# Attention and two MoE layers on one core: the activations of five tiles turned in 32x32 blocks by VectorE instead of by TensorE

## Chip, cores and metric

The kernel runs on one core of one Trainium2 chip. The metric is the device time of one execution in microseconds (us). PE is TensorE, PEld its weight loads, DVE VectorE, ACT ScalarE, POOL GpSimd, SP the engine whose queue issues most transfers.

## What is computed

Three layers follow each other (batch 4, 8 heads, 512 local and 32 global positions, head size 64, so 2176 rows of 512):

```
out_g = softmax(scale * q_g @ [k_g, k_l].T) @ [v_g, v_l]              # global rows
s_l   = scale * [q_l @ k_g.T, where(|i - j| <= 32, q_l @ k_l.T, -1e9)] # local rows
out_l = softmax(s_l) @ [v_g, v_l]
x = rows of [out_g, out_l]                       # 2176 x 512

h = x @ w_in                                     # 2176 x 2048
g = maximum(0.01 * h, h)
x = g @ w_out                                    # 2176 x 512

logits = x @ phi                                 # 2176 x 32, 8 experts x 4 slots
d = softmax(logits, axis=0)                      # over all rows
slot_out[e] = maximum((d.T @ x)[e] @ w1[e], 0) @ w2[e]
out = softmax(logits, axis=1) @ slot_out
```

## The kernel before

The rows are worked in 17 tiles of 128 (`NTT`): four per batch, 0 to 15, and tile 16 with the global rows. The attention of a batch (`a_T`, `a_S`, `a_E`, `a_V`, `g_S`, `g_E`, `g_V`) fills `xn`; the MLP of its tiles runs beside the attention of the next batch.

For one tile t the MLP does the following.
- `b_X` (L635) turns x on TensorE and splits it into two parts, `xh` and `xl`.
- `b_H` (L657) makes one slice f of h, 512 of the 2048 columns, by 12 matmuls into a bank `hp` (two banks), and ScalarE's activation writes g (L679).
- `b_L` (L683) turns that slice of g: four transposes on TensorE (L688) into a bank, and one copy (L690) to a tile `gT`. From tile 6 on that copy is ScalarE's.
- `b_M` (L695) multiplies all four `gT` of a tile with `pmat`, which is w_out @ phi made ahead, so that logits come without x @ w_out: 16 matmuls (L700) into one bank `lg`, columns by four row groups.
- `b_D1` copies `lg` to `lp` on VectorE (L709), `b_D2` adds the four groups on TensorE (L715, `lg<-lp`) and takes the running column maximum and exponentials, `b_D3` turns them back (L759, `lg<-identr,st`) and makes the row softmax.
- `b_U` adds d.T @ g to a sum over tiles (`up`, L769; `uacc`, L774).

`l_items(t)` lists the steps after H of one tile, `b_items` weaves those of tile t-1 between the H slices of tile t. Tiles 15 and 16 (`ts`) are done together at the end (`j_M`, `j_D`). The order on each engine is set by the framework's scheduler from the order of the code, from dependences and from a simulated timeline; `tc.issue_after(ins)` adds the edge that what follows is issued after `ins`. The semaphores and the buffers of the pools make the waits. A pool tile with a tag has `bufs` buffers that are used in turn; `reuse_waits="tile"` lets a new tile wait for all users of the one it replaces.

The experts' weights, 33.5 MB, are loaded by `load_next`, in the order of a list `loads`, as buffers come free: eight of pool `xp`, the eight of `wp` (the parts of w_in, each pair free after H of its slice for tile 16), those of `g`, `xn`, `xh` and `xl`. They are used by `layer1` (`ehp`, L1113) and the second layer (`sop`).

Of the kernel before, what the change touches and what calls it, by code (L numbers as in the profile page):

```python
# [20 lines left out]
def kernel(  # L21
# [20 lines left out]
    P = 128  # L42
# [68 lines left out]
    st = actx.enter_context(tc.tile_pool(name="st", bufs=2))  # L111
# [3 lines left out]
    m32 = sb.tile([32, 3, P], F32, tag="gT", name="m32", bufs=4)  # L115
# [87 lines left out]
    def load_vn(b):  # L203
# [8 lines left out]
        vnat[b] = (t, g)  # L212

# [93 lines left out]
    def p_items():  # L307
# [23 lines left out]
        def chunk(c, j):  # L331
# [4 lines left out]
            wt = sb.tile([P, 4, P], F32, tag="gT", name="wt", bufs=4)  # L336
            nc.scalar.copy(wt.rearrange("p d f -> p (d f)"), ps_t)
            wts[j] = wt
# [244 lines left out]
    def g_load(src):  # L583
        t = sb.tile([P, H, D], F32, tag="gT", name="gn", bufs=4)
# [48 lines left out]
    seq = [(b, T) for b in range(B) for T in range(NT)] + [None]  # L633

# [22 lines left out]
    def b_H(t, f, half=None):  # L657
# [21 lines left out]
        nc.scalar.activation(out=gs, in_=hp, func=AF.Prelu, alpha=0.01)  # L679

    lst = {}

    def b_L(t, f, ev=None):  # L683
        g = gt[t]
        pt = tp("gtp")
        for c in range(4):
            o = 512 * f + P * c
            nc.tensor.transpose(pt[:, P * c:P * c + P], g[:, o:o + P], ident)  # L688
        gT = sb.tile([P, 4, P], F32, tag="gT", name="gT", bufs=4)
        (ev or (nc.vector.tensor_copy if f % 2 and not (t >= 6 and f in (1, 3, 9)) else nc.scalar.copy))(  # L690
            gT.rearrange("p c t -> p (c t)"), pt
        )
        lst[t, f] = gT

    def b_M(t):  # L695
        lg = bank("sm", "lg", 1)
        for f in range(NQ):
            gT = lst.pop((t, f))
            for c in range(4):
                nc.tensor.matmul(  # L700
                    lg[32 * c:32 * c + 32, 0:P], pmat[:, c, f, :], gT[:, c, :],
                    start=(f == 0), stop=(f == NQ - 1), skip_group_check=True,
                )
        return lg

    def b_D1(t):
        lg = b_M(t)
# [221 lines left out]
    xb.append(bctx.enter_context(tc.tile_pool(name="xb", bufs=1, side="right")))  # L929
    for x in l_items(2):  # L930
# [22 lines left out]
    xp = bctx.enter_context(tc.tile_pool(name="xp", bufs=8))  # L953
# [39 lines left out]
    BUFS = {"x": 8, "y": 2, "w": 8, "xn": 1, "g": 2}  # L993
# [30 lines left out]
    load_next(*[xs] * 4)  # L1024
# [248 lines left out]
```

## Time and profile before

| | us |
|---|---|
| median of 3 runs | 524.31 |
| lowest, highest | 524.26, 526.5 |
| span of the profiled execution | 522.1 |

The span reaches from the first to the last instruction of the profiled execution; the time of a run also has what lies around it. The profiled execution's own time is not among the numbers, so its span stands beside the median, 2.2 us above.

| engine | busy us | share of the span |
|---|---|---|
| PE | 479.9 | 92% |
| PEld | 337.1 | 65% |
| DVE | 251.4 | 48% |
| ACT | 245.0 | 47% |
| POOL | 83.4 | 16% |

A share is an average over three stages: attention with the conversion of w_in and w_out (to about 140 us), attention beside the MLP (to about 340 us), and the MLP alone with the experts behind it. Matmuls overlap in the pipeline, so that a group's mean is longer than the step from one matmul to the next; the chain of waits shows that step. In the chain PE has 66% of the span, the largest line of it L672, the matmuls of `b_H`.

### The profile page before, as it was taken

How to read it: one execution, taken by the hardware profiler on the slowest of the kernel's cores; microseconds unless marked ns; L12 is line 12 of the kernel's file. 1: busy time of each engine (PE TensorE's matmuls, PEld its weight loads, DVE VectorE, ACT ScalarE, POOL GpSimd, SP SyncE). 2: the span in 40 equal slices, each digit the busy share in tenths (PEclk: the TensorE clock that was granted, in tenths of full speed). 3: DMA queues.
4: the chain of work that ended last, by engine and by line, in shares of the span. 5: the costliest groups of instructions: out<-in, count | busy, mean ns of one | idle time of the engine just before them, and what ended most of it. 6: DMA issues, size and time to landing. Idle time of an engine off the chain costs nothing.

```text
span 522.1 us, 13688 instructions
## 1 busy us (share of the span) xinstructions
PE 479.9 (92%) x5455; PEld 337.1 (65%) x5455; DVE 251.4 (48%) x901; ACT 245.0 (47%) x747; POOL 83.4 (16%) x103
## 2 busy tenths in 40 slices
PE   7966988988999889999999999999999999999991
PEld 5744666556765667677767775767787777633371
DVE  4585769778486683735453354313222212312441
ACT  4687889779445353622462535143424334300231
POOL 2054788453102010010110101000000000000000
PEclk9968899999998999999999999999999999999997
DMA  9998778799554654124250220269500258999977
GB/s 178 216 226 225 205 218 305 207 323 276 148 126 81 169 97 89 41 55 135 45 102 4 52 55 3 82 237 404 206 1 1 82 181 278 360 361 380 318 222 221
DMA packets 122396, 90.26 MB, mean 173 GB/s; under 512 B 75804, under 2 KB 101212, under 8 KB 122332
## 3 DMA queue, kind: packets, MB, share of 16 engines
q1 hardware_dynamic: 119660, 88.33, 59.6%
q10 hardware_dynamic: 2672, 1.05, 0.8%
q8 instruction: 43, 0.70, 0.6%
q14 instruction: 21, 0.17, 0.1%
HBM read 76.68 MB, written 8.65 MB: 163 GB/s over the span
## 4 chain that ended last, share of the span: by engine, by line
PE 66%; DVE 8%; DMA 8%; ACT 7%; SPq 4%; issue 3%; POOL 1%; ACTq 0%; POOLq 0%; DVEq 0%
PE hp L672 30%; PE gtp L688 6%; DMA rraw<-in_moe_w_in_dram 4%; PE ehp L1113 3%; PE up L769 3%; PE lg L700 3%; PE po L480 3%; PE sc L423 3%; DMA rraw<-in_moe_w_out_dram 2%; ACT se L443 2%; SPq L162 2%; PE etp L462 2%; PE sop L1167 1%; SPq L222 1%; DVE se L435 1%
## 5 line engine op out<-in xcount | busy, mean ns | idle before, releaser
L672 PE MATMUL hp<-wi,xxh 128*128 128x512 f32 x512 | 167.1, 407 | 4.7 <-ACT g L679 2.9
L672 PEld LDWEIGHTS hp<-wi,xxh 128*128 128x128 f32 x512 | 93.0, 191 | 33.8 <-issue 8.8
L672 PE MATMUL hp<-wi,xxl 128*128 128x512 f32 x256 | 101.9, 399 | 0.0
L679 ACT ACTIVATE g<-hp 128x512 f32<-128x512 f32 x60 | 34.9, 592 | 66.3 <-PE hp L672 64.2
L443 ACT ACTIVATE se<-se,nmx 128x128 f32<-128x128 f32 x128 | 49.6, 390 | 22.5 <-DVE nmx L441 22.4
L672 PEld LDWEIGHTS hp<-wi,xxl 128*128 128x128 f32 x256 | 48.6, 190 | 11.8 <-issue 0.8
L690 ACT COPY gT<-gtp 128x512 f32<-128x512 f32 x56 | 31.5, 588 | 30.1 <-PE gtp L688 27.7
L200 POOL COPY vw<-vw 32x1664 f32<-32x1664 f32 x10 | 15.7, 1574 | 165.3 <-DMA vw<-in_v_g_dram 129.3
L688 PE MATMUL gtp<-identr,g 128*128 128x128 f32 x240 | 35.4, 279 | 1.8 <-ACT gs L529 1.2
L688 PEld LDWEIGHTS gtp<-identr,g 128*128 128x128 f32 x240 | 26.8, 141 | 9.7 <-issue 2.8
L250 POOL TENSOR_TENSOR wn<-wn,rraw 128x256 int32<-128x256 int32 x32 | 26.0, 828 | 33.5 <-ACT wn L239 24.4
L435 DVE CUSTOM_DVE_ANT_0 se<-sc,mask 128x128 f32<-128x128 f32 x128 | 29.0, 283 | 3.8 <-PE sc L423 3.7
L423 PE MATMUL sc<-kw,qT 64*32 64x128 f32 x1024 | 28.8, 284 | 0.0
L464 DVE COPY eT<-etp 128x512 f32<-128x512 f32 x28 | 18.7, 687 | 20.1 <-PE etp L462 19.9
L240 ACT ACTIVATE rraw<-rraw 128x256 int32<-128x256 uint32 x55 | 23.5, 436 | 5.7 <-DMA rraw<-in_moe_w_in_dram 4.5
L480 PE MATMUL po<-vw,eT 128*32 128x64 f32 x1024 | 23.1, 227 | 2.1 <-DMA vw<-vw 1.5
L462 PE MATMUL etp<-identr,se 128*128 128x128 f32 x128 | 21.9, 294 | 2.8 <-DVE gT L690 1.4
L443 ACT ACTIVATION_READ_ACCUMULATOR se<-se,nmx 128x1 f32 x128 | 24.1, 188 | 0.0
L423 PEld LDWEIGHTS sc<-kw,qT 64*32 64x32 f32 x1024 | 19.9, 109 | 6.0 <-issue 3.3
L480 PEld LDWEIGHTS po<-vw,eT 128*32 128x32 f32 x1024 | 18.1, 113 | 8.7 <-issue 8.1
L250 POOL TENSOR_TENSOR wo<-wo,rraw 128x256 int32<-128x256 int32 x23 | 18.5, 820 | 22.4 <-ACT wo L239 5.5
L394 DVE COPY kw<-kT 128x672 f32<-128x672 f32 x32 | 18.9, 627 | 5.8 <-ACT kT L383 5.7
(221 smaller groups left out, 750.6 us busy)
## 6 DMA issues: line engine op xcount, KB each, us to landing
ew<-in_moe_w_dram SPq DMA_DIRECT2D x23, 1024.0 KB, 8.7
rraw<-in_moe_w_in_dram SPq DMA_DIRECT2D x32, 256.0 KB, 3.6
vw<-in_v_l_dram SPq DMA_DIRECT2D x60, 112.0 KB, 3.3
rraw<-in_moe_w_out_dram SPq DMA_DIRECT2D x23, 256.0 KB, 5.3
ew<-in_moe_w_dram SPq DMA_DIRECT2D x9, 512.0 KB, 9.8
ew<-in_moe_w_dram SPq DMA_DIRECT2D x17, 256.0 KB, 5.5
wo_f<-wo SPq DMA_DIRECT2D x16, 256.0 KB, 4.6
vn<-in_v_l_dram SPq DMA_DIRECT2D x4, 1024.0 KB, 6.8
```

Of the source, the lines that this page charges most:

```text
L240: nc.scalar.activation(out=m, in_=lo, func=AF.Copy, scale=2.0 ** -29)
L250: nc.gpsimd.tensor_tensor(out=di, in0=di, in1=m, op=ALU.add)
L394: nc.vector.tensor_copy(kw[:, :, 0:96], src)
L423: nc.tensor.matmul(bks[e][32 * u:32 * u + 32, P * T:P * T + P], qt[64 * e:64 * e + 64, 32 * U:32 * U + 32], kw[win(U) // (NW // 2)][64 * e ...
L435: nc.vector.tensor_tensor_reduce(out=s[:, T, :], in0=bk[:, P * T:P * T + P], in1=mask[:, 0 if T == 0 else 2 if T == NT - 1 else 1, :], sca ...
L443: exp_last[0] = nc.scalar.activation(out=s[:, T, :], in_=s[:, T, :], func=AF.Exp, bias=nmx[:, e, T:T + 1], accum_out=sm[:, T, e:e + 1],).ins
L462: nc.tensor.transpose(pt[:, P * T:P * T + P], es[e][:, T, :], ident)
L480: nc.tensor.matmul(pov[32 * u:32 * u + 32, T, e, :], ets[e][:, 32 * U:32 * U + 32], vw[:, win(U), e, :], start=True, stop=True,)
L672: nc.tensor.matmul(hp, a[:, k, :], w[c][:, k, :], start=(k == 0 and n == 0), stop=(k == KD - 1 and n == 2),)
L679: nc.scalar.activation(out=gs, in_=hp, func=AF.Prelu, alpha=0.01)
L688: nc.tensor.transpose(pt[:, P * c:P * c + P], g[:, o:o + P], ident)
L690: (ev or (nc.vector.tensor_copy if f % 2 and not (t >= 6 and f in (1, 3, 9)) else nc.scalar.copy))(gT.rearrange("p c t -> p (c t)"), pt)
```

## The change

Tiles 10 to 14 (`BLK`) no longer use `b_L`. After each activation of a slice `blocks` turns it in 32x32 blocks on VectorE into one half of a tile `gb`; after the second slice of a pair 16 copies of 32 partitions move the blocks to their places in `g8`. Slices 0 and 1 have all 16 on GpSimd, slices 2 and 3 have 6 on GpSimd, 5 on VectorE, 5 on ScalarE (`MOVE`). `b_M` takes these halves, the first of them before the rest as an item of its own; `behind` makes some H slices be issued after an instruction of the logits' chain (`ms["b"]`). For the buffers, tag `gT` has two tiles of double size whose halves `part` hands out, pool `st` moves to the other end of the memory and is given back earlier, `xp` has 7 buffers, and one load of expert weights (`held`) is made later, into the place of `g8`.

```diff
+    BLK = range(10, NTT - 2)
+    MOVE = "P" * 16, "PPPPPPDDDDDAAAAA"
...
         nc.scalar.activation(out=gs, in_=hp, func=AF.Prelu, alpha=0.01)
+        if t in BLK:
+            blocks(t, f, gs)
...
+    def blocks(t, f, gs):
+        if f % 2 == 0:
+            gbl[0] = sb.tile([P, 2, 512], F32, tag="gT", name="gb", bufs=2)
+            gbl[1] = gp[0].tile([P, 2, 4, P], F32, tag="g8", name="g8", bufs=2)
+        gb, g8 = gbl[0], gbl[1]
+        nc.vector.transpose(out=gb[:, f % 2], in_=gs)
+        lst[t, f] = g8[:, f % 2]
+        if f % 2 == 0:
+            return
+        src = gb.rearrange("p f (q c j) -> p (f q) c j", c=4, j=32)
+        dst = g8.rearrange("p f q (a j) -> p (f q) a j", j=32)
+        for n in range(16):
+            a, c = n // 4, (n + n // 4) % 4
+            copy = {"P": nc.gpsimd.tensor_copy, "A": nc.scalar.copy, "D": nc.vector.tensor_copy}[MOVE[f // 2][n]]
+            copy(dst[32 * c:32 * c + 32, :, a], src[32 * a:32 * a + 32, :, c])
...
+    def b_M(t, fs=range(NQ)):
+        if 0 in fs:
+            ms["M"] = bank("sm", "lg", 1)
+        lg = ms["M"]
+        for f in fs:
...
     def b_D1(t):
-        lg = b_M(t)
+        lg = b_M(t, range(2, NQ) if t in BLK else range(NQ))
...
+    def behind(item):
+        def go():
+            with tc.issue_after(ms["b"]):
+                item[1]()
+        return (item[0], go) + item[2:]
...
+            if t - 1 in BLK:
+                its += h[0:2] + [li[1]] + h[2:4] + [li[2]] + x + [behind(h[4])]
+                its += [li[3]] + [behind(x) for x in h[5:8]] + [li[4], li[5]]
+                continue
...
-    st = actx.enter_context(tc.tile_pool(name="st", bufs=2))
+    st = pctx.enter_context(tc.tile_pool(name="st", bufs=2, side="right"))
-    xp = bctx.enter_context(tc.tile_pool(name="xp", bufs=8))
+    xp = bctx.enter_context(tc.tile_pool(name="xp", bufs=7))
...
-    load_next(*[xs] * 4)
+    load_next(*[xs] * 3)
+    held = loads.pop(0)
...
-    run(H(ts[0], 0), li[0], X(ts[1]), H(ts[1], 0), li[1])
+    run(H(ts[0], 0), X(ts[1]), li[1], H(ts[1], 0), li[2])
...
-    run(H(ts[0], 1), li[2], H(ts[1], 1, 0), li[3], H(ts[1], 1, 1), li[4])
-    load_next(ws, ws)
-    run(H(ts[0], 2), li[5])
+    gctx.close()
+    gctx = ExitStack()
+    g8s = (gctx.enter_context(tc.tile_pool(name="ge", bufs=1, side="right")), "e8")
+    run(behind(H(ts[0], 1)), li[3], behind(H(ts[1], 1)), li[4])
+    loads.insert(0, held)
+    load_next(g8s, ws, ws)
+    run(behind(H(ts[0], 2)), li[5])
```

TensorE, the logits of a tile in the middle of the stretch. Before (`gT` is the turned g, `hp` the H matmuls of the next tile; the `lg<-lp` of this tile follows 21 of them):

```order
L688 MATMUL gtp<-identr,g 128x128 x3
L769 MATMUL up<-g,d 32x512 [waits DVE_49]
L769 MATMUL up<-g,d 32x512 x3
L700 MATMUL lg<-gT,pmat 32x128 [waits Activation_49]
L700 MATMUL lg<-gT,pmat 32x128 x7
L642 MATMUL xtp<-identr,xn 128x128 [waits Activation_49]
L642 MATMUL xtp<-identr,xn 128x128 x3
L700 MATMUL lg<-gT,pmat 32x128 x4
L700 MATMUL lg<-gT,pmat 32x128 [waits Activation_49]
L700 MATMUL lg<-gT,pmat 32x128 x3
L672 MATMUL hp<-wi,xxh 128x512 [waits Activation_49]
```

TensorE, the same place in the changed kernel (`g_5227` and `g_5315` are the two `g8` of one tile):

```order
L654 MATMUL xtp<-identr,xn 128x128 x3
L735 MATMUL lg<-g_5227,pmat 32x128 [waits Activation_49,Pool_49]
L735 MATMUL lg<-g_5227,pmat 32x128 x7
L735 MATMUL lg<-g_5315,pmat 32x128 [waits DVE_49,Activation_49,Pool_49]
L735 MATMUL lg<-g_5315,pmat 32x128 x7
L684 MATMUL hp<-wi,xxh 128x512 [waits Activation_49]
L684 MATMUL hp<-wi,xxh 128x512
L684 MATMUL hp<-wi,xxl 128x512
L684 MATMUL hp<-wi,xxh 128x512 x2
L684 MATMUL hp<-wi,xxl 128x512
L750 MATMUL lg<-lp,s_77 128x128 [waits DVE_49]
```

The transposes and `up` are no longer ahead of the logits, whose halves now wait for the block copies, and `lg<-lp` stands 6 matmuls behind them instead of 21.

VectorE, around `lp` of one tile. Before:

```order
L774 SCALAR_TENSOR_TENSOR uacc<-uacc,al,up 128x512 [waits PE_49]
L709 COPY lp<-lg 128x128 [waits PE_49]
L719 TENSOR_REDUCE nm<-lg 128x1 [waits PE_49]
L723 TENSOR_TENSOR nm<-nm 128x1 [waits DVE_49]
L728 TENSOR_TENSOR al<-nm 128x1 [waits DVE_49]
```

VectorE, the same place in the changed kernel (`gb` are the transposed blocks, `g_5623` a `g8`):

```order
L712 COPY g_5623<-gb 32x8x32 x4
L789 RECIPROCAL cs<-cs 128x1 [waits DVE_49]
L790 TENSOR_SCALAR cnat<-ce,cs 128x32 [waits DVE_49]
L810 SCALAR_TENSOR_TENSOR uacc<-uacc,al,up 128x512 [waits PE_49]
L703 STREAM_TRANSPOSE gb<-g 128x512 [waits Activation_49,Pool_49]
L703 STREAM_TRANSPOSE gb<-g 128x512 [waits Activation_49]
L744 COPY lp<-lg 128x128 [waits PE_49]
L754 TENSOR_REDUCE nm<-lg 128x1 [waits PE_49]
```

Two block transposes of the next tile's slices now stand ahead of `lp`, each waiting for its activation.

SP, the queue of the expert loads where the MLP ends. Before (`128x2x1024` is a piece of w1, `128x4x512` one of w2, 1 MB each):

```order
L967 DMA ew<-in_moe_w_dram 128x2x1024 [waits DMAHW0_49,PE_49]
L974 DMA ew<-in_moe_w_dram 128x4x512 [waits DMAHW1_49,PE_49]
L974 DMA ew<-in_moe_w_dram 128x4x512 [waits DMAHW2_49,PE_49]
L974 DMA ew<-in_moe_w_dram 128x4x512 [waits DMAHW3_49,PE_49]
L974 DMA ew<-in_moe_w_dram 128x4x512 [waits DMAHW4_49,PE_49]
```

SP, the same place in the changed kernel:

```order
L1016 DMA ew<-in_moe_w_dram 128x2x1024 [waits DMAHW7_49,PE_49]
L1023 DMA ew<-in_moe_w_dram 128x4x512 [waits DMAHW0_49,PE_49]
L1016 DMA ew<-in_moe_w_dram 128x2x1024 [waits DVE_49,PE_49,DMAHW1_49,Activation_49,Pool_49]
L1023 DMA ew<-in_moe_w_dram 128x4x512 [waits DMAHW2_49,PE_49]
L1023 DMA ew<-in_moe_w_dram 128x4x512 [waits DMAHW3_49,PE_49]
```

The held piece stands between the two pieces freed by slice 0 and the two freed by slice 1, and waits for all users of the `g8` memory.

## Rows read from the trace of the kernel before

**Rows 1.** Busy time by stretch: stretch, length, engines, clock, DMA share, GB/s.

```profile
400.00:420.00 20.00, 20.00 (x135) 15.92 (x134) 5.26 (x19) 8.16 (x21) 0.00 (x0) 1.00 0.21 66
...
440.00:460.00 20.00, 19.36 (x163) 11.98 (x166) 7.08 (x28) 5.71 (x15) 0.00 (x0) 1.00 0.99 354
...
480.00:500.00 20.00, 19.28 (x189) 7.60 (x183) 6.35 (x11) 3.44 (x8) 0.00 (x0) 1.00 1.12 316
```

**Rows 2.** Chain of waits, one tile's cycle: start us, us, what.

```profile
392.01 1.00 PE up L769 x8
...
394.03 0.57 PE lg L700 x16
394.60 4.99 PE hp L672 x21
...
400.51 0.87 PE gtp L688 x8
401.39 2.75 PE hp L672 x12
...
407.00 0.87 PE gtp L688 x8
407.88 0.99 PE up L769 x8
```

**Rows 3.** Chain of waits, the last wait for expert weights.

```profile
494.81 5.45 DMA ew<-in_moe_w_dram
```

**Rows 4.** Groups of the page: line engine op out<-in xcount | busy, mean ns | idle.

```profile
L690 ACT COPY gT<-gtp 128x512 f32<-128x512 f32 x56 | 31.5, 588 | 30.1 <-PE gtp L688 27.7
...
L688 PE MATMUL gtp<-identr,g 128*128 128x128 f32 x240 | 35.4, 279 | 1.8 <-ACT gs L529 1.2
L688 PEld LDWEIGHTS gtp<-identr,g 128*128 128x128 f32 x240 | 26.8, 141 | 9.7 <-issue 2.8
...
L464 DVE COPY eT<-etp 128x512 f32<-128x512 f32 x28 | 18.7, 687 | 20.1 <-PE etp L462 19.9
L240 ACT ACTIVATE rraw<-rraw 128x256 int32<-128x256 uint32 x55 | 23.5, 436 | 5.7 <-DMA rraw<-in_moe_w_in_dram 4.5
```

**Rows 5.** VectorE by source line: count, shortest/median/longest ns, first and last start.

```profile
L395 DVE COPY kw<-kgT x32: 267/276/819, 8.4 to 306.5; 128x224 f32<-128x224 f32 x32
...
L242 DVE TENSOR_SCALAR wo<-wo x32: 270/292/867, 79.7 to 132.9; 128x256 uint32<-128x256 uint32 x32
```

**Rows 6.** Instructions in order of time, GpSimd and VectorE at 60 us.

```profile
60.10 1.90 POOL L250 TENSOR_TENSOR wn<-wn,rraw 128x256 int32<-128x256 int32 x2
...
60.12 1.28 DVE L299 TENSOR_TENSOR wi<-wn,wi 128x512 fp32r<-128x512 f32 x1 [0.77 <-ACT wi L298]
```

**Rows 7.** Groups of GpSimd.

```profile
L250 POOL TENSOR_TENSOR wn<-wn,rraw 128x256 int32<-128x256 int32 x32 | 26.0, 828 | 33.5 <-ACT wn L239 24.4 <-DVE wn L246 3.9 <-DMA rraw<-in_moe_w_in_dram 2.2
...
L200 POOL COPY vw<-vw 32x1664 f32<-32x1664 f32 x10 | 15.7, 1574 | 165.3 <-DMA vw<-in_v_g_dram 129.3 <-PE gtp L688 19.9 <-PE hp L672 16.1
```

**Rows 8.** Instructions in order of time, logits and a slice's activation.

```profile
409.82 0.65 PE L700 MATMUL lg<-gT,pmat 128*32 128x128 f32 x16
...
410.54 0.29 DVE L709 COPY lp<-lg 128x128 f32<-128x128 f32 x1 [0.85 <-PE lg L700]
...
413.02 0.39 PE L672 MATMUL hp<-wi,xxl 128*128 128x512 f32 x1
...
413.45 0.60 ACT L679 ACTIVATE g<-hp 128x512 f32<-128x512 f32 x1 [2.92 <-PE hp L672]
```

**Rows 9.** DMA share by stretch of 2 us, and the SP queue.

```profile
429.00:431.00 2.00, 2.00 (x10) 1.64 (x9) 0.04 (x1) 0.00 (x0) 0.00 (x0) 1.00 0.32 120
431.00:433.00 2.00, 2.00 (x15) 1.74 (x15) 0.00 (x0) 1.08 (x2) 0.00 (x0) 1.00 0.13 42
...
423.11 15.93 SPq L974 DMA_DIRECT2D ew<-in_moe_w_dram  x5
```

**Rows 10.** Chain of waits, its first piece.

```profile
0.81 3.40 DMA kn<-in_k_l_dram
```

More of the change, by code (lines that the diff above doesn't have):

```diff
@@ L212, in load_vn, with part @@
         vnat[b] = (t, g)
+    spare = []
+    def part(name, dt=F32):
+        if not spare:
+            t = sb.tile([P, 2, 512], dt, tag="gT", name=name, bufs=2)
+            spare.extend((t[:, 1], t[:, 0]))
+        return spare.pop()
     def words(w):
@@ L335, in chunk @@
                 nc.tensor.transpose(ps_t[:, P * d:P * d + P], wo[:, P * d:P * d + P], ident)
-            wt = sb.tile([P, 4, P], F32, tag="gT", name="wt", bufs=4)
-            nc.scalar.copy(wt.rearrange("p d f -> p (d f)"), ps_t)
-            wts[j] = wt
+            wt = part("wt")
+            nc.scalar.copy(wt, ps_t)
+            wts[j] = wt.rearrange("p (d f) -> p d f", d=4)
         def prod(c):
@@ L583, in g_load @@
     def g_load(src):
[L584 removed]
+        t = sb.tile([P, H, D], F32, tag="gT", name="gn", bufs=2)
         for b in range(B):
@@ L688, in b_L @@
             nc.tensor.transpose(pt[:, P * c:P * c + P], g[:, o:o + P], ident)
-        gT = sb.tile([P, 4, P], F32, tag="gT", name="gT", bufs=4)
+        gT = part("gT")
         (ev or (nc.vector.tensor_copy if f % 2 and not (t >= 6 and f in (1, 3, 9)) else nc.scalar.copy))(
-            gT.rearrange("p c t -> p (c t)"), pt
+            gT, pt
         )
[L693 to L697, printed above, removed]
+        lst[t, f] = gT.rearrange("p (c t) -> p c t", c=4)
+    def b_M(t, fs=range(NQ)):
[3 more added lines that the diff above has]
+        for f in fs:
             gT = lst.pop((t, f))
             for c in range(4):
-                nc.tensor.matmul(
+                ms["b"] = nc.tensor.matmul(
                     lg[32 * c:32 * c + 32, 0:P], pmat[:, c, f, :], gT[:, c, :],
                     start=(f == 0), stop=(f == NQ - 1), skip_group_check=True,
-                )
+                ).ins
         return lg
     def b_D1(t):
-        lg = b_M(t)
+        lg = b_M(t, range(2, NQ) if t in BLK else range(NQ))
         lp = sb.tile([P, 2 * P], F32, tag="lp", name="lp", bufs=1)[:, 0:P]
@@ L827, in l_items @@
     def l_items(t):
-        return [
+        return ([(0.0, lambda: None), (0.6, lambda: b_M(t, range(2)))] if t in BLK else [
             (0.9, lambda: (b_L(t, 0), b_L(t, 1))),
             (0.9, lambda: (b_L(t, 2), b_L(t, 3))),
+        ]) + [
             (1.3, lambda: b_D1(t)),
@@ L1079 @@
         ).ins
-    uT = small("gT", [P, 4, 4, NS], "uT")
-    uTf = uT.rearrange("p c j s -> p (c j s)")
+    uTf = part("uT")
+    uT = uTf.rearrange("p (c j s) -> p c j s", c=4, j=4)
     nc.vector.tensor_copy(uTf[:, 0:256], pts[0][:, 0:256])
@@ L1092 @@
         load_next(xs)
-    si = small("gT", [P, 512], "si")
+    si = part("si")
     nc.vector.tensor_scalar_mul(si[:, 0:256], sip[:, 0:256], rz)
@@ L1121, in layer1 @@
             if (r, k, n) == (0, 3, 1):
-                load_next(xs)
+                load_next(g8s)
         hzT = []
         for n in range(2):
-            hz = small("gT", [P, 512], "hz")
+            hz = part("hz")
             nc.vector.tensor_scalar(
```

19 lines of the change are left out of this document (12 added, 7 removed).

## Prediction

> **What bounds the kernel now.** I read the busy shares by stretch first, then the chain of waits, then the DMA queue. While the MLP tiles run, TensorE is busy in every microsecond at full clock, VectorE, ScalarE and DMA have room, and GpSimd does nothing: the stretch from 400 us shows it [rows 1]. One tile's cycle, from one `up` product to the next, takes 407.88 - 392.01 = 15.87 us, and every piece of it is TensorE's [rows 2]. So there a matmul saved is time saved, and a matmul that waits is time lost. From 440 us on the DMA engines are full as well [rows 1]: they bring the expert weights, and the last thing that TensorE waits for is such a load, 5.45 us [rows 3]. The end therefore moves only if the loads move with TensorE.
>
> **What is removed.** For tiles 10 to 14, `b_L` no longer turns g: 5 tiles x 4 slices x 4 = 80 transposes leave TensorE, and 20 evictions of 128x512 (588 ns, [rows 4]) leave ScalarE. What a transpose is worth needs a choice. Its mean of 279 ns counts overlapping work [rows 4]; 80 of them would be 22 us. In the chain eight take 0.87 us, 0.109 us each [rows 2], since the next one enters before the last has left. I take the chain: 80 x 0.109 = **8.7 us**, or 2 x 0.87 = 1.74 us of each 15.87 us cycle, which leaves 14.1. The Trainium skill ("Trainium Kernel Development and Optimization", Performance Expectations) calls matmul busy time a bad metric because matmuls are pipelined, and weight-load time a good one. By it the sum would be 80 x 26.8/240 us [rows 4] = 8.9 us; the trace agrees, since that is the chain's figure and not the 22.
>
> **What is added beside TensorE.** Per tile:
> - VectorE: 4 block transposes of 128x512. No row shows one. Nearest is a 128x512 copy at 687 ns [rows 4]; below it a 128x224 copy within SBUF at 267 ns, 0.61 us for 512 columns in proportion [rows 5]; above it the same size with two inputs beside GpSimd, 1.28 us [rows 6]. I take 0.69, the same size with one input. Its 5 block copies (32x256): the 128x224 copy gives 0.3 us each.
> - ScalarE: 5 copies at the 436 ns of a 128x256 one [rows 4] = 2.2 us, for 4 x 0.59 = 2.4 us removed.
> - GpSimd: 22 copies of 32x256. The 32x1664 copy took 1574 ns [rows 7], so 0.24 us in proportion; the two-input 128x256 operation 828 ns [rows 7]. I take 0.33, near the copy with something for the start of each: 22 x 0.33 = 7.3 us per tile, all in time where it was idle.
>
> In sum VectorE gets 4 x 0.69 + 5 x 0.3 = 4.3 us more in a cycle of 14.1, and at 5.26 of 20 us [rows 1] it has the room. None of this costs TensorE time unless a result comes late. There are three such places, and the order of the instructions says what TensorE does meanwhile.
>
> *The two halves of the logits (`b_M`).* TensorE's first half waits for GpSimd's 16 copies of slices 0 and 1, the second half for the 6 + 5 + 5 of slices 2 and 3. Behind the last matmul of a tile come the H slices 0 and 1 of the next tile, 12 matmuls in 2.75 us each, `up` at 0.99 and the first half at 0.57 [rows 2]: 7.06 us. Before the second half can start the chain is: the activation, which ends 1.03 us after the slice's last matmul began (413.02 to 413.45 + 0.60, [rows 8]) and so 0.8 us after the next work entered TensorE 0.229 us later; the block transpose behind an `xxl` subtraction of the same size, 2 x 0.69 = 1.4; then 6 GpSimd copies, 2.0, or 5 on ScalarE, 2.2. That is 4.4 us, and 2.6 us are over. The first half has a whole cycle: 22c on GpSimd must fit in 14.1 us, so a copy may take up to c = 0.64 us.
>
> *The column sums (`lg<-lp`).* These now stand 6 matmuls behind the logits, 6 x 2.75/12 = 1.38 us, where 21 stood [rows 2]. The copy `lp` starts 0.07 us after the last logit and takes 0.29 [rows 8], but on VectorE it is now queued behind the block transpose of slice 1 of the next tile, which waits for its activation. From the end of that slice: activation at +0.2 to +0.8, transpose to +1.5, lp to +1.8; TensorE comes after two halves of logits at 2 x 0.57 + 1.38 = +2.5. No wait, 0.7 us over; a transpose above 1.4 us would begin to cost.
>
> *The other queues.* ScalarE's 5 copies wait for the transpose of slice 3 and hold the activation of the next slice 0; that is wanted only by H slice 2, some 4 us later. I cost all of these at nothing.
>
> **Who shares a port.** A VectorE subtraction beside GpSimd took 1.28 us while GpSimd had two operations in a row [rows 6], and a 128x256 operation within SBUF reached 867 ns from 270 [rows 5]: VectorE waits for one GpSimd instruction and then goes. Here that is 0.33 us for each of the two short two-input operations between the column sums and the transposed softmax, which stand 18 matmuls apart, 4.1 us. And the 5 + 6 copies of slices 2 and 3 on these two engines may run one after the other: 1.5 us more before the second half of the logits, of the 2.6 that are over. I take no cost, and count it to rival 1. The Trainium skill ("SBUF — State Buffer", Who interferes with whom) says that a VectorE copy in a two-port mode, or an operation with two SBUF inputs, and a GpSimd operation exclude each other for the whole instruction, and whoever starts second blocks. It speaks against sharing these copies between the two. By it the copies would always take the 1.5 us, by the rows alone none or all of it; the trace agrees on the wait, and no row shows these copies.
>
> **The tail.** One of the first four expert pieces is held back (xp has 7 buffers), 1 MB that loads after tile 14's logits into the moved blocks' buffers. At 354 GB/s [rows 1] it is 3.0 us more in the full stretch; or nothing, if it fits where the DMA idles now: its share is 0.32 and 0.13 in the four microseconds from 429 [rows 9], between the weight pieces freed by H slice 0 and those freed by slice 1. The held load stands in the queue just there, behind the pair whose second is issued at 423.11 [rows 9]. That hole is 2 x (0.68 + 0.87) = 3.1 us, so I take nothing. The release times of these buffers come earlier by 6.9 to 8.7 us (72 to 80 transposes saved before them, `up` of tile 13 or 14, 0.99 us, moved ahead of some). After that each load follows a TensorE event, and all events of the tail move by 8.7.
>
> **The start.** The first kn load now waits for VectorE's copy of the identity (the buffers moved), and two loads of a later head go first. The chain there runs through that queue's wait for its first load, 3.40 us [rows 10]; the first load still goes at once and four are out before the wait, as now. Bounds: -0.2 to +1; I take +0.2. The 0.5 MB piece of `xe` loads in the attention of the second batch, ahead of its vw, instead of after the last: 0 to 1.5 us by the rate above, of which I take 0 and keep the rest for the range.
>
> **Sum.** -8.7 + 0 (waits) + 0 (held load) + 0.2 = -8.5 us. The profiled execution: span 522.1 to 513.6. The median of the runs is 524.31, 2.2 above that span, and the same 2.2 stays: **515.8 us**.
>
> **Rivals.**
> 1. *The loads do not follow, or small waits appear (part of the gain).* The held MB costs its 3.0 us: 518.8. Or the blocks of slices 2 and 3, or lp behind its transpose, come 0.5 us late in four tiles: 2 us, 517.8. Both: 520.8. For it: DMA at 0.99 and more from 440 us [rows 1]; against it: the hole [rows 9].
> 2. *GpSimd becomes the bound (slower).* Twelve of the 16 blocks go to other partitions than they come from, and no row shows GpSimd doing that. If a copy took the 0.83 us of the two-input row, a cycle would be 22 x 0.83 = 18.3 us; four cycles lie between the logits of tile 10 and of tile 14: 4 x (18.3 - 15.87) - 1.74 = +8, so 532.3 us. It decides from 0.74 us a copy on (4 x (22c - 15.87) = 1.74). Against it: one input instead of two, and the copy row's 0.24.
> 3. *It does not do what it says (no change).* The transposes go, but TensorE waits as long for the blocks: copies of 0.72 us give 4 x 22 x 0.72 - 4 x 15.87 - 1.74 = -1.9, about 522.5; so also if the early loads lose several microseconds.
>
> **How the numbers follow.** Forecast 0.68 (514 to 517.5), rival 1 0.15 (517.5 to 521), rival 2 0.09, rival 3 0.08. The range from 513.5 to 521 takes in the first two, 0.83. About 0.5% (2.6 us) is what a measurement of this kernel can tell from no change, so faster by more is under 521.7: 0.83; within it 0.08; slower 0.09.
>
> **What would show it.** Right: a cycle of 13.4 to 14.1 us from `up` to `up`; TensorE at 20 of 20 us from 360 us to the end of the tiles; 22 GpSimd copies near 0.33 us ending well ahead of their logits; the last DMA wait still 5 us, 8.5 us earlier. Wrong: idle of TensorE before `lg<-g8` with GpSimd as releaser (rival 2), before `lg<-lp` with VectorE's lp (rival 1), or a last DMA wait that has grown by 3 us.

## The result and the profile after

The changed kernel takes 517.78 us (median of 4 runs, 515.66 to 521.94) against 524.79 (4 runs, 524.26 to 526.5): a ratio of 0.9861, interval 0.9813 to 0.9909. The forecast was 515.8, the range 513.5 to 521.0. The profiled execution is one of 515.66 us; its span went from 522.1 to 513.9 us, where the prediction's sum had 513.6. That agreement is partly luck, as the next paragraph shows.

The first 215 us take several us more or less from run to run, with the stretches in which TensorE's granted clock is below 1.00, and in the profiles below that share the code of that start the `up` product of tile 3 begins anywhere from 212.20 to 218.80 us. So I compare kernels from that `up` to the end of the span, where the clock of both kernels stays at 1.00 until the output stage. The two rows of the chain of waits (start us, us, what) and the spans, first of before, then of after:

```profile
215.18 0.99 PE up L769 x8
...
core 0: 522.1 us, clock 0.973
```

```profile
213.85 0.99 PE up L805 x8
...
core 0: 513.9 us, clock 0.978
```

Before, 522.1 - 215.18 = 306.9 us lie behind it, after 513.9 - 213.85 = 300.05. So from there on the change is worth **6.9 us**, and the other 1.3 us of the profiled spans are an earlier start, well within the 6.6 us by which that start varies.

Busy time by stretch in the kernel after; the columns are those of [rows 1]:

```profile
340.00:360.00 20.00, 18.71 (x148) 13.93 (x136) 8.42 (x23) 8.14 (x19) 8.68 (x22) 1.00 0.88 330
...
380.00:400.00 20.00, 20.00 (x123) 14.33 (x122) 12.62 (x34) 9.31 (x26) 13.73 (x35) 1.00 0.01 2
...
420.00:440.00 20.00, 20.00 (x127) 15.05 (x126) 3.55 (x13) 5.98 (x14) 0.00 (x0) 1.00 1.01 367
```

TensorE still bounds the tiles: 20.00 of 20 us, as in [rows 1], while VectorE and GpSimd now work beside it. Two things are new: TensorE idles 1.3 us where the turned tiles begin (340 to 360 us), 0.9 us more than before, where it was busy for 19.58 of these 20; and the DMA share is 1.01 from 420 us on, where the queue had holes before [rows 9].

One tile's cycle in the chain of waits of after, which answers to [rows 2]:

```profile
385.08 1.00 PE up L805 x8
386.08 2.95 PE hp L684 x12
389.03 1.01 PE lg L735 x32
390.04 1.59 PE hp L684 x6
391.63 0.22 PE lg L750 x2
391.85 4.13 PE hp L684 x18
395.98 0.11 PE lg L795
396.09 2.75 PE hp L684 x12
398.84 1.00 PE up L805 x8
```

From `up` to `up` it is 13.76 us where [rows 2] had 15.87, every piece TensorE's. The eight transposes that stood twice in [rows 2] are gone. So are 0.59 us of `xtp`: the X of four tiles stands in earlier cycles now. A likely reason, which no run tests, is that the transposes of g used the same two banks (tag `tp`) and are gone. Either way it is moved work, no gain. A cycle of after that has its `xtp` takes 385.08 - 370.90 = 14.18.

What the added instructions cost, by source line (count, shortest/median/longest ns, first and last start):

```profile
L712 POOL COPY g<-gb x110: 390/395/768, 344.3 to 413.9; 32x256 f32<-32x256 f32 x110
L712 ACT COPY g<-gb x25: 400/402/405, 353.4 to 413.3; 32x256 f32<-32x256 f32 x25
L712 DVE COPY g<-gb x25: 281/419/507, 354.7 to 413.2; 32x256 f32<-32x256 f32 x25
...
L703 DVE STREAM_TRANSPOSE gb<-g x20: 670/704/712, 342.9 to 410.9; 128x512 f32<-128x512 f32 x20
```

The block transpose was put at 0.69 us and took 0.70. GpSimd's copy was put at 0.33; it took 0.40, and 16 in a row took 6.94, so 0.43 with the step from one to the next. VectorE's was put at 0.3 and took 0.42, ScalarE's at 0.44 and took 0.40.

### The profile page after: what moved, and what is told of

Same layout as the page of the kernel before. It is cut to its first block, busy times and chain, and to the rows that moved or that the text cites. A ratio compares the mean times of both kernels' runs of the same rounds, so it can differ in the third digit from the quotient of the medians.

```text
span 513.9 us, 13696 instructions
## 1 busy us (share of the span) xinstructions
PE 475.0 (92%) x5375; PEld 328.3 (64%) x5375; DVE 275.4 (54%) x946; ACT 246.2 (48%) x752; POOL 126.6 (25%) x213
## 4 chain that ended last, share of the span: by engine, by line
PE 65%; DVE 11%; DMA 9%; ACT 5%; issue 3%; SPq 3%; POOL 2%; ACTq 0%; POOLq 0%; DVEq 0%
PE hp L684 31%; DMA rraw<-in_moe_w_in_dram 4%; PE gtp L721 4%; PE ehp L1167 3%; PE lg L735 3%; PE up L805 3%; PE po L489 3%; PE sc L432 3%; DMA rraw<-in_moe_w_out_dram 2%; PE etp L471 2%; POOL wn L259 2%; DVE se L444 2%; PE sop L1243 1%; PE sop L1221 1%; SPq L162 1%
## 5 line engine op out<-in xcount | busy, mean ns | idle before, releaser
L712 POOL COPY g<-gb 32x256 f32<-32x256 f32 x110 | 44.1, 401 | 55.8 <-DVE gb L703 47.0
L723 ACT COPY gT<-gtp 128x512 f32<-128x512 f32 x36 | 20.7, 586 | 19.8 <-PE gtp L721 14.2
L721 PE MATMUL gtp<-identr,g 128*128 128x128 f32 x160 | 24.4, 281 | 2.0 <-ACT gs L538 1.4
L721 PEld LDWEIGHTS gtp<-identr,g 128*128 128x128 f32 x160 | 17.5, 140 | 8.3 <-issue 2.2
```

What stands on the lines that cost most here:

```text
L712: copy(dst[32 * c:32 * c + 32, :, a], src[32 * a:32 * a + 32, :, c])
```

## The experiments

In all edits the kernel is the changed one but for the lines shown. "Stretch" is the time from the `up` of tile 3 to the end of the span, in the profiled execution. There is one such profile per kernel. After and e3, whose waits of TensorE differ by 0.3 us, lie 0.1 us apart in it. The part from the `wm` group (eight warm-up products that begin behind the last tiles' logits, at 452.38 us before) to the end is 69.7 us before and after, and 68.9 to 70.3 us over the kernels of the table, so that tenths of the stretch are not always the tiles'. "Rest" is what the median moved against the runs of before on the same chip (medians 523.6 to 524.8) beyond what the stretch moved; it holds the start and the spread.

| kernel | median us (runs) | ratio to before, interval | stretch us | rest us |
|---|---|---|---|---|
| before | 524.79 (4) | | 306.92 | |
| after | 517.78 (4) | 0.9861, 0.9813 to 0.9909 | 300.05 | -0.1 |
| e1, nothing turned | 526.11 (10) | 1.0054, 1.0018 to 1.0090 | 307.18 | +1.4 |
| e2, tiles 12 to 14 | 523.16 (10) | 0.9983, 0.9939 to 1.0026 | | |
| e3, no copy on VectorE | 516.44 (4) | 0.9862, 0.9805 to 0.9919 | 300.16 | -1.3 |
| e4, all copies on GpSimd | 524.06 (10) | 0.9996, 0.9959 to 1.0033 | 305.84 | +0.7 |
| e5, own memory for the first gb | 516.46 (4) | 0.9813, 0.9747 to 0.9880 | 298.78 | +0.4 |
| e6, held load left out | 518.38 (4) | 0.9868, 0.9813 to 0.9923 | 299.16 | +2.0 |
| e7, tiles 8 to 14 | 514.59 (4) | 0.9801, 0.9742 to 0.9860 | 296.87 | +0.5 |
| e8, no order edges | 546.66 (4) | 1.0406, 1.0349 to 1.0464 | 329.74 | -0.3 |
| e9, tiles 6 to 14 | 520.28 (10) | 0.9943, 0.9900 to 0.9985 | 304.30 | -0.9 |
| e10, tiles 4 to 14 | 527.50 (10) | 1.0068, 1.0030 to 1.0105 | | |
| e11, `up` later | 519.64 (10) | 0.9901, 0.9866 to 0.9936 | 299.42 | +3.3 |
| e12, e3 + e7 + e11 | 515.51 (6) | 0.9855, 0.9820 to 0.9889 | 296.07 | +2.8 |

### e1: the turning alone undone

```
-    BLK = range(10, NTT - 2)
+    BLK = ()
-    run(H(ts[0], 0), X(ts[1]), li[1], H(ts[1], 0), li[2])
+    run(H(ts[0], 0), li[0], X(ts[1]), li[1], H(ts[1], 0), li[2])
```

> The turning alone is undone: no tile is in BLK, so all of g is turned on TensorE again and the logits keep their old order; the pool changes, the half buffers for the turned g, 7 xp buffers and the held expert piece stay. My theory (80 transposes of 0.109 us off a stretch that TensorE bounds, with loads that follow): the whole gain of 8.7 us goes, 524 to 526.5 us, cycles from up to up of 15.9 us. Rival (part of the gain comes from the moved pools, loads and their earlier release): 518 to 522 us. Rival (the held piece costs its 3.0 us and the turning hid that): 527 to 529 us.

Measured: 526.11 us, the stretch 307.18, against 306.92 before; cycles of 15.87 us (391.88 - 376.01). The whole gain goes with the turning: my theory stands, and the gain is in the turned tiles. Up to the `wm` group the stretch is 236.96 us in e1 (451.88 - 214.92), 237.20 before (452.38 - 215.18) and 230.41 after (444.26 - 213.85), so the other parts of the change give some 0.2 of the 6.8 us there.

For the tail and the start e1 is not the clean comparison that I had meant. With no `g8` in use, the place of the held load is free early: a 1 MB piece of w1 (L1016) is issued at 137.3 us already, where the changed kernel has the first of them at 344.3. So the rival on the held piece is not tested here. And behind `wm` TensorE waits 1.27 us for an expert load (0.33 before), and its granted clock is 0.66 from 500 to 505 us where before has 1.00.

The median lies 0.5% above before, by more than its interval, and the stretch does not show it; what is left is in the start and its spread (+1.4 us of rest), where this early load falls as well.

### e2: three tiles

```
-    BLK = range(10, NTT - 2)
+    BLK = range(12, NTT - 2)
```

> Only tiles 12 to 14 are turned in blocks, tiles 10 and 11 on TensorE. My theory (1.74 us per tile, in proportion): 2 x 1.74 = 3.5 us more than the changed kernel, 519.5 to 521.5 us; the wait for the xxl subtraction where the first turned tile begins (0.5 us) moves to tile 12 with it. Rival (the gain is made by the release of the tail's buffers, which follows tiles 12 to 14 alone): 517 to 518.5 us.

Measured: 523.16 us over a wide spread (519.67 to 527.58), more than expected. Its profile is of a run that was late already at tile 8, so I read only from the `up` of tile 8 to the warm-up products that begin behind the last tiles' logits (the `wm` group): 110.02 us before, 109.63 in e1, 107.59 here, 103.07 after. Three tiles give 2.0 us against e1, and the two more of the changed kernel 4.5. So the gain is not in proportion to the tiles: the entry into the turned tiles costs, here 1.5 us of waits that the trace names (0.7 for an activation, 0.5 for `xxl`, 0.3 for `d`). The other 1.7 us that are missing from the expected 5.2 I could not place. The rival (all gain from the buffers' release) falls: e2 releases them as the changed kernel does.

### e3 and e4: who moves the blocks

```
-    MOVE = "P" * 16, "PPPPPPDDDDDAAAAA"
+    MOVE = "P" * 16, "PPPPPPPPPPPAAAAA"      (e3)
+    MOVE = "P" * 16, "P" * 16                (e4)
```

> The 5 block copies of slices 2 and 3 on VectorE go to GpSimd, which then has 11 there and ScalarE its 5. My theory, with 0.43 us per GpSimd copy (16 in 6.95 us in the changed kernel): activation and transpose end 2.2 us after H slice 3, 11 x 0.43 = 4.8, together 7.0 of the 7.2 us until the second half of the logits: no wait of TensorE or at most 0.3 us per tile, 517 to 519.5 us. Rival 1 (GpSimd is already the late one): 5 x 0.43 = 2.2 us more per tile, 10 us more, 527 us. Rival 2 (copies of VectorE and GpSimd shut each other out, so that sharing gains nothing): no change, and GpSimd copies beside an idle VectorE are shorter, below 0.38 us each.

> All 16 block copies of slices 2 and 3 go to GpSimd as those of slices 0 and 1 do: 32 x 0.43 = 13.9 us per tile in a cycle of 13.8. My theory: 2.2 + 16 x 0.43 = 9.1 us after H slice 3 against 7.2 that are covered, so TensorE waits 1.4 to 2 us for the second half of the logits in each of 5 tiles: 7 to 10 us, 524.5 to 528 us, idle of TensorE at the logits with GpSimd as releaser. Rival (GpSimd's idle time in the cycle hides them all): within 1 us of the changed kernel, 517 to 519 us.

Measured: e3 is the changed kernel again (stretch 300.16), e4 is 5.8 us worse (305.84), somewhat less than expected. The waits of TensorE in e4 between 342 and 445 us (who waited for whom, us in total, times, longest us):

```profile
PE lg L735 <- POOL g L712: 5.0, 4, 1.5
```

and two of its instructions in order of time:

```profile
375.46 0.65 PE L735 MATMUL lg<-g,pmat 128*32 128x128 f32 x16 [1.49 <-POOL g L712]
...
390.93 0.64 PE L735 MATMUL lg<-g,pmat 128*32 128x128 f32 x16 [1.50 <-POOL g L712]
```

This comes near rival 2 of the prediction: 32 copies per tile put GpSimd on the path, TensorE waits up to 1.5 us for the second half of the logits, and the cycle is 390.93 - 375.46 = 15.5 us. GpSimd is not full even so: its 32 copies take 13.94 us of that cycle, and for 1.5 us it waits for the blocks. What counts is the chain behind slice 3. e3 is still short of that point: by the expectation 2.2 + 11 x 0.43 = 7.0 of the 7.2 us are used, in its trace the eleven copies end at 383.94 + 4.74 = 388.68, ahead of both halves of the logits (from 388.85 on), and TensorE has no such wait. The chain that the prediction set up for the second half (activation, block transpose, copies) says rightly at 6, 11 and 16 copies whether TensorE waits, and at 16 it is 0.4 us too long (9.1 - 7.2 = 1.9 for 1.5).

e3 also speaks on the shared port. GpSimd's copies are no shorter beside an idle VectorE, so there my rival 2 falls:

```profile
L712 POOL COPY g<-gb x135: 390/394/769, 344.3 to 415.9; 32x256 f32<-32x256 f32 x135
```

It is VectorE that pays, 0.42 us where its shortest copy took 0.28. That GpSimd is the reason, e9's trace shows: there VectorE's five copies took 0.29, 0.39, 0.43, 0.28 and 0.28 us, the last two from 263.50 on, and GpSimd's six ended at 260.44 + 2.90 = 263.34. But the two do not run one after the other. In the changed kernel, in order of time:

```profile
384.04 2.00 DVE L712 COPY g<-gb 32x256 f32<-32x256 f32 x5
384.06 2.06 ACT L712 COPY g<-gb 32x256 f32<-32x256 f32 x5 [0.68 <-DVE cs L788]
384.13 2.63 POOL L712 COPY g<-gb 32x256 f32<-32x256 f32 x6 [0.80 <-DVE cs L788]
```

Five and six copies take 2.63 us together; one after the other they would take 5 x 0.28 + 6 x 0.43 = 4.0. The rule that the prediction weighed (the Trainium skill, "SBUF — State Buffer", Who interferes with whom: a VectorE copy in a two-port mode and a GpSimd operation exclude each other for the whole instruction) would have made it so, if these copies run in such a mode, which no run shows. The trace agrees in that VectorE's copies get longer beside GpSimd, and not on the whole instruction.

### e5: the entry into the turned tiles

```
-            gbl[0] = sb.tile([P, 2, 512], F32, tag="gT", name="gb", bufs=2)
+            gbl[0] = (sa.tile([P, 2, 512], F32, tag="vw", name="gb", bufs=2) if (t, f) == (10, 0)
+                      else sb.tile([P, 2, 512], F32, tag="gT", name="gb", bufs=2))
```

> The first gb of tile 10 gets memory of its own (a buffer of the attention's V, idle by then) instead of one of the two buffers that it shares with the turned g of tile 9. My theory (the idle time of TensorE where the turned tiles begin comes from this sharing: the eviction gT at 349.8 us waits for logits of tile 9, the block transpose behind it does too, and the xxl subtraction is queued behind both): the waits for xxl (0.54 us) and d (0.28 us) in the first cycle go, 18.86 us from up(8) to up(9) become about 18.0, all else the same; about 0.9 us of time, within the spread of the median, 515.5 to 518 us. Rival (the wait comes from the order of VectorE, block transposes ahead of lp and xxl, whatever the memory): the same idle time as in the changed kernel.

First the place, in the chain of waits of the changed kernel:

```profile
349.81 0.60 ACT gT L723
...
351.82 0.71 DVE gb L703
352.53 0.18 DVE lp L744
...
353.32 0.59 DVE xxl L661
...
353.95 4.83 PE hp L684 x20
```

The eviction gT of tile 9 starts only when the logits before it have freed the buffer (TensorE's transposes for it ended at 349.1), because gb of tile 10 holds the other of the two. The third block transpose then waits for tile 9's last logits, and lp and xxl stand behind it on VectorE. TensorE idles 0.54 us for xxl and later 0.28 for `d`. The waits of TensorE in this stretch, of the changed kernel, then of e5:

```profile
PE hp L684 <- DVE xxl L661: 0.5, 1, 0.5
PE up L805 <- DVE d L782: 0.3, 1, 0.3
```

```profile
PE up L806 <- DVE d L783: 0.3, 1, 0.3
```

The wait for xxl is gone, that for `d` stays, which my theory had wrong. The cycle from the `up` of tile 8 to that of tile 9 falls from 18.86 to 17.71 us, more than the 0.9 expected: beside the 0.54 us of idle time the steps next to it get shorter (20 H matmuls in 4.57 us for 4.83). The stretch falls by 1.27 to 298.78, of which 1.06 lie ahead of `wm` (446.97 - 217.62 = 229.35 for 230.41). So most of the entry cost is the shared memory, and it is worth 1.1 to 1.3 us.

### e6: the held load

```
-    loads.insert(0, held)
-    load_next(g8s, ws, ws)
+    load_next(ws, ws)
+    w1t[held[1], held[2]] = w1t[held[1], 0]
```

> The load of the held expert piece (1 MB) is left out, and the layer that wants it reads another piece of the same expert; nothing else is changed. My theory (the held load fits a stretch where the DMA has room): 0 to 0.5 us less than the changed kernel, 516 to 518 us, the loads from 435 us on issued at the same times. Rival (it costs its 3.0 us in the full stretch): 513 to 515 us, and the DMA waits of the second expert layer 3 us shorter or gone.

Measured: the stretch is 299.16, 0.9 us shorter. The held load and the last loads in SP's queue (start us, us from first to last issue), of after and of e6:

```profile
418.89 0.37 SPq L1016 DMA_DIRECT2D ew<-in_moe_w_dram  x1
...
461.28 27.68 SPq L1035 DMA_DIRECT2D ew<-in_moe_w_dram  x21
```

```profile
422.76 0.92 SPq L1035 DMA_DIRECT2D ew<-in_moe_w_dram  x2
...
465.14 25.49 SPq L1035 DMA_DIRECT2D ew<-in_moe_w_dram  x19
```

Counted from the `up` of tile 3, these issues end at 275.1 us in after and at 465.14 + 25.49 - 217.94 = 272.7 in e6. But e6 does not leave the place of the held load empty: two of the 21 loads behind it, 1 MB together, which use the same buffer later in the changed kernel, are issued there at 422.76 us. So e6 shows what one megabyte less in the full stretch is worth to the last loads, 2.4 us, and not whether the held one fits the hole. Nor are the 0.9 us surely the load's: TensorE waits for no expert load behind 450 us in either kernel, and in the output stage, where 0.7 of them arise, the products stand in another order in e6. Neither the theory nor the rival is settled by this run.

What the changed kernel itself shows speaks for the hole. Between the issues of the pairs freed by slice 0 and by slice 1 lie 424.51 - 416.36 = 8.15 us. By the rate of [rows 1] (an estimate) the first pair takes 5.9 us and the held load 3.0, so that some 0.7 us stand over. And the last loads end as much earlier as TensorE's work: before, 469.12 + 28.11 - 215.18 = 282.1 us from that `up`, after 275.1, a difference of 7.0 us where the stretch falls by 6.9.

### e7, e9 and e10: more tiles

```
-    BLK = range(10, NTT - 2)
+    BLK = range(8, NTT - 2)     (e7)
+    BLK = range(6, NTT - 2)     (e9)
+    BLK = range(4, NTT - 2)     (e10, with e3's MOVE)
```

> Tiles 8 and 9 are turned in blocks as well, whose H slices run beside the attention of the last batch. My theory (TensorE bounds that stretch too, at 20.0 of 20 us from 220 to 340 us but for 18.6 around 310, and GpSimd copies take 9.5 us per tile where it was idle but for 1.6 us): 2 x 1.74 = 3.5 us less, 513 to 515 us. Rival (VectorE and ScalarE have the attention's softmax in their queues there; block transposes and copies ahead of it make TensorE wait by as much or more): 517 to 521 us, idle of TensorE before the attention's products or the logits of tiles 8 and 9.

> Tiles 6 and 7 are turned in blocks as well, so nine tiles, 6 to 14; the first of them lie beside the attention of the third batch. My theory (1.74 us per tile wherever TensorE is busy throughout, less some tenths for waits): from the `up` at about 214 us to the end 296.87 us with tiles 8 to 14; two more tiles make it 293.4 to 294.5 us, and the median 511 to 513 us. Rival (with the attention's softmax on VectorE and ScalarE the waits eat the two tiles' gain): 296.5 to 299 us for the stretch, 514 to 517 us.

> All tiles from 4 to 14 are turned in blocks, and the 5 copies of slices 2 and 3 that were VectorE's go to GpSimd, since VectorE is the busier of the two beside the attention. My theory: four tiles more than 8 to 14, 4 x 1.74 = 7 us less some tenths for waits, 290 to 291.5 us from the `up` at about 214 us to the end (296.87 with tiles 8 to 14), and the median 508 to 510 us. Rival (the attention's softmax, queued behind block transposes and copies on VectorE and ScalarE, makes TensorE wait): above 294 us, idle of TensorE with ScalarE or VectorE as releaser between 215 and 340 us.

Measured: two tiles more give 3.2 us of the 3.5 expected (296.87). Four more do not: e9's stretch is 304.3, above the changed kernel's, beyond even the rival's range; e10 is slower than before, 527.5 us. (In e10 the tile of the reference `up` lies beside turned tiles, so it has no comparable stretch.) Busy time by stretch in e9, and pieces of its chain of waits there:

```profile
260.00:265.00 5.00, 2.75 (x76) 2.13 (x77) 4.88 (x14) 3.23 (x9) 2.69 (x6) 1.00 0.98 163
265.00:270.00 5.00, 4.53 (x59) 3.25 (x61) 4.94 (x29) 2.52 (x10) 1.58 (x1) 0.53 0.02 3
```

```profile
258.28 0.71 DVE gb L703
258.99 0.58 DVE xxl L661
...
264.08 0.61 DVE eT L473
```

VectorE is full (4.88 of 5 us): from 258.28 to 264.08 us the chain is its queue, block transposes, xxl, the attention's kw and five block copies, and at its end eT, which the attention's products need. TensorE is busy for 2.75 of these 5 us, and in the next five the granted clock is 0.53 where the changed kernel has 1.00 throughout, so nearly all of them at the lower of its two levels, 1.2 GHz. In e10 the longest waits are 4.2 us for `st`, 2.4 for `kT` and 1.9 for `mx`, mostly VectorE's. ScalarE has its part too: the longest wait in e9 is 3.1 us, for its `gs`, which itself waited for VectorE's maximum. The rival's mechanism is what happened, and the fall of the clock adds to its price. But it is not the softmax alone: tiles 8 and 9, beside the attention of the last batch, lost only 0.3 of their 3.5 us (e7). Of the 20 us from 260 VectorE is busy for 13.0: it has room in the mean and none where it counts.

### e8: the order edges

```
-            with tc.issue_after(ms["b"]):
-                item[1]()
+            item[1]()
```

> The order edges (behind) are taken out; everything else stays. TensorE's order is then, for each turned tile, logits, column sums, transposed softmax and up in a row, with no H matmuls between. My theory (the edges earn nothing themselves, but the turned tiles need H work between these four steps): TensorE waits per tile for lp (0.4 us), max, exp and the copy of st (1.2 us), and d (0.3 us), some 2 us in each of 5 tiles, 10 us more than the changed kernel, 525 to 530 us. Rival (the edges are only a matter of form, the stretch is bound by TensorE's work in any order): 516 to 519 us.

Measured: 546.66 us, 29 us more than the changed kernel, where I had expected 10. The waits of TensorE from 360 to 445 us:

```profile
PE lg L795 <- DVE st L760: 8.7, 4, 2.8
PE hp L684 <- ACT g L691: 2.4, 4, 0.7
```

With 1.1 us for `d` and 0.8 for lp they are 13 us, near the 10. A part that I had not counted is that VectorE's five block copies come between lp and nm. Most of the rest is the clock: from 375 to 455 us its mean is 0.83, which at two levels of 1 and 0.5 is 27 us at the lower one, and half of them, some 13.6 us, is what TensorE's work loses there at most (an estimate). With the waits that makes 26.6 of the 29.7 us by which the stretch grew. By stretch, with the mean granted clock ahead of the DMA share:

```profile
420.00:425.00 5.00, 3.28 (x11) 1.16 (x12) 3.23 (x11) 1.90 (x7) 4.48 (x13) 0.50 0.02 5
425.00:430.00 5.00, 5.00 (x13) 3.84 (x13) 0.49 (x1) 0.34 (x1) 1.16 (x3) 0.50 0.00 0
```

and in its chain 24 H matmuls behind such a gap:

```profile
381.66 7.74 PE hp L684 x24
```

They take 7.74 us where 24 took 5.47 in e11. In 425 to 430 us TensorE is busy throughout, at half clock, the 1.2 GHz level; in the 5 us from 415, ahead of that fall, it was busy for 2.47. So the edges earn their place: they put H matmuls where VectorE and ScalarE work.

### e11: where the rest went

```
-                nc.tensor.matmul(
+                ms["h"] = nc.tensor.matmul(
...
+    def late(item):
+        def go():
+            with tc.issue_after(ms["h"]):
+                item[1]()
+        return item[0], go
...
-                its += h[0:2] + [li[1]] + h[2:4] + [li[2]] + x + [behind(h[4])]
-                its += [li[3]] + [behind(x) for x in h[5:8]] + [li[4], li[5]]
+                its += h[0:2] + [li[1]] + h[2:4] + up + [li[2]] + x + [behind(h[4])]
+                its += [li[3]] + [behind(x) for x in h[5:8]] + [li[4]]
+                up = [late(li[5])]
```

> In the changed kernel, `up` of tiles 10 to 12 moves behind H slice 1 of the tile after next to it in TensorE's order, so that it stands right ahead of the logits, as in the kernel before; nothing else is changed. My theory (the 12 H matmuls behind `up` took 2.95 us in the chain and 12 in mid-run 2.75; the 0.2 us are paid at each change from 32-column products back to H, and the changed kernel has one such change more per cycle, which is where 0.9 us of the 8.7 went): the cycle from logits to logits falls from 13.76 to 13.55 us, in all 0.6 us, not to be seen in the median of 515.5 to 518 us. Rival (the 0.2 us belong to the H matmuls of that slice, whatever stands ahead of them): 13.76 us as before.

One cycle in its chain of waits:

```profile
392.31 0.99 PE up L805 x8
393.31 0.87 PE lg L735 x32
...
400.34 5.47 PE hp L684 x24
405.81 0.99 PE up L805 x8
```

It is 405.81 - 392.31 = 13.50 us, 0.26 less than in the changed kernel with the same instructions, and the stretch is 299.42, 0.63 less (expected 0.6). In the changed kernel, in order of time, with the array's form behind the names:

```profile
385.01 1.07 PE L805 MATMUL up<-g,d 128*32 128x512 f32 x8
386.01 0.73 PE L684 MATMUL hp<-wi,xxh 128*128 128x512 f32 x2
386.58 0.39 PE L684 MATMUL hp<-wi,xxl 128*128 128x512 f32 x1
386.81 0.62 PE L684 MATMUL hp<-wi,xxh 128*128 128x512 f32 x2
387.27 0.40 PE L684 MATMUL hp<-wi,xxl 128*128 128x512 f32 x1
```

The first pair of H matmuls behind the 128x32 products takes 0.57 us to the next row, a later pair 0.46. The logits do the same, 1.01 us behind H and 0.87 right behind `up`. The Trainium skill ("TensorEngine Tiling (Array Packing)", Key Properties) says that a change of tiling mode drains TensorE; the trace agrees, at 0.1 to 0.15 us for a change each way. The change had moved `up` away from the logits, of the same form, and so made two more of these per cycle wherever no `xtp` stood between.

### e12: the best of it together

The edits of e3, e7 and e11.

> Three edits together: tiles 8 to 14 turned in blocks (from `up` at 215.03 us to the end 296.87 us, against 300.05 of the changed kernel), `up` right ahead of the logits (0.26 us per cycle, in all cycles but the last one), and no block copy on VectorE (nothing in itself; where tiles 8 and 9 lie beside the attention, TensorE waited 1.7 us for xxl and st, which VectorE makes). My theory, that the three add up: 296.87 - 5 x 0.26 = 295.6 us for that stretch, down to 294 if VectorE's shorter queue takes the two waits away; the median some 4.5 to 6 us under the changed kernel's, 511.5 to 515 us. Rival (GpSimd's 27 copies per tile come late beside the attention, or `up` moved back holds a g buffer too long): 297 us or more for the stretch, idle of TensorE before the logits with GpSimd as releaser.

Measured: the stretch is 296.07, 4.0 us under the changed kernel's; 0.5 us of the sum did not come, and with 27 copies per tile GpSimd stands in its chain of waits. The median, 515.51, and that of e7, 514.59, lie under the changed kernel's 517.78, but the intervals of the ratios overlap. Both beat the kernel before beyond doubt; that they beat the changed one is shown by the stretch alone.

## Why the prediction was right, and where it was not

**The bound and the price of a transpose: right.** TensorE bounds the tiles, and the rate of the chain, 0.109 us [rows 2], was the right one. Against e1 the stretch fell by 307.18 - 300.05 = 7.1 us; with the 1.27 us of e5 and the 0.63 of e11, which the change lost elsewhere, that is 9.0, against 80 x 0.109 = 8.7. Counted only to the `wm` group, where e1's own tail has no part, it is 236.96 - 230.41 = 6.55, and with 1.06 and 0.67 of e5 and e11 (448.22 - 218.48 = 229.74) 8.3. The mean of 279 ns of [rows 4] would have said 22.

**"None of this costs TensorE time unless a result comes late. There are three such places": there is a fourth.** At the three places named nothing waited: the copies of the second pair ended at 384.13 + 2.63 = 386.76, 2.8 us ahead of the second half of the logits (2.6 forecast), and no `lg<-lp` waited for lp. But I followed the turned tiles in their steady cycle and not the one cycle in which tile 9 is still turned the old way while tile 10 takes one of the two half buffers. That is 1.1 to 1.3 us (e5), and it was there to be read in the diff, in the `bufs=2` of the tag that gT and gb share.

**`up` moved at no cost: wrong by 0.6 us.** [rows 2] shows `up` and logits in one run; I moved `up` away in the count of the cover and did not ask what the change of form costs (e11). The sum of the three is 8.7 - 1.27 - 0.63 = 6.8; measured 6.9. That it closes to 0.1 us is in part luck, since each of these terms comes from one profile and the same sum for e12 missed by 0.5.

**GpSimd's copy: mis-sized, without effect.** 0.43 us in place of 0.33 makes 22 copies 9.5 us per tile, of 13.8. The limits that the prediction gave (0.64 for no wait, 0.74 for slower than before) were far enough off. e4 shows, with 32 copies, that GpSimd can come onto the path, though by the chain behind slice 3 and not by being full. Of the 1.5 us that two engines shutting each other out could have cost, 0.6 came: VectorE's five copies took 2.0 us in place of 5 x 0.28 = 1.4, within the time that was over.

**The tail: the end followed, one reading is open and two failed.** From the `wm` group to the end it is 69.7 us before and 69.6 after, so the loads did follow TensorE. That the held load costs nothing is not shown, since neither e1 nor e6 takes that load alone; what the changed kernel shows (e6) speaks for it. The release times come earlier by less than the 6.9 to 8.7 us forecast: the first pair of the tail is issued 416.36 - 213.85 = 202.5 us behind the `up` of tile 3, before 422.64 - 215.18 = 207.5, so 5.0 us. And the "last DMA wait still 5 us" is no longer in the chain. Of the 5.45 us of [rows 3] TensorE had idled only 0.33, as its instructions in order of time show in the kernel before:

```profile
500.31 1.06 PE L1190 MATMUL sop<-ew,hzT 128*32 128x128 f32 x26 [0.33 <-DMA ew<-in_moe_w_dram]
```

The rest of that piece had other products beside it. In the changed kernel they stand in another order there, the output products first, and TensorE waits for none of these loads.

**The start: mis-sized, if anything.** I put it at +0.2 us, between -0.2 and +1. The column of the rest is, over the eleven kernels that have one, 0.8 us in the mean, from -1.3 to +3.3. So the moved loads and buffers of the start may cost about 1 us, but the spread of the start, 212 to 219 us for the same code, does not let me say it, and no run here took that part alone (e1 has the held load in its start as well).

**So the time.** The forecast's 8.5 was 1.6 too much for what the change does behind the start; the profiled run hid that with a start 1.3 us earlier, and the median, 517.78, shows it. The mechanism was the likeliest case's, and the time lies just above that case's own band (514 to 517.5), where rival 1 (small waits appear) had put it, though the waits were at another place than it named.

## What to carry to other kernels

When an engine that bounds a stretch gives work away, its gain is read from its chain, at the rate at which instructions follow each other there; what is lost again is read from the edges, from the first and last tile of the new kind, where old and new share a ring of buffers, and from what the moved instructions stood next to. Spread the added work until the chain that feeds the bounding engine fits its cover (here 7.2 us), not until the other engines are level: 11 copies on one engine cost nothing, 16 cost 5.8 us over five tiles. And where the engine that takes the work has a softmax of its own in its queue, try it tile by tile: two tiles beside the last batch gave 3.2 us (e7), two more lost 7.4 (e9), and room in the mean told nothing of it.

## What the hardware showed beyond that

- **Idle time of TensorE can be paid twice.** Some 13 us of waits in e8 went with 29 us of time, since the granted clock fell to 0.50 behind them (24 H matmuls in 7.74 us against 5.47); in e9 it fell to 0.53 behind 5 us in which TensorE was busy for 2.75. It need not be so: behind the four waits of e4, of up to 1.5 us, the clock stayed at 1.00.
- **Products in the form 128x32 next to products in the form 128x128** cost 0.1 to 0.15 us at each change, 0.26 us per cycle (e11).
- **GpSimd moves a 32x256 f32 block to other partitions** at 0.40 us, 0.43 in a row, and no slower beside VectorE; VectorE's copy goes from 0.28 to 0.42 beside it, and neither waits for the other's whole run (five and six of them in 2.63 us).
